# A transformer layer's first loads in another order: Q and K weights first on one queue, two x tiles on the scalar queue, no touching read

## The chip, the cores and the metric

The kernel runs on one core of one Trainium2 chip. A core has five engines that run side by side, each in the order of its own program: TensorE (PE, matmuls and transposes, its weight loads shown as PEld), VectorE (DVE), ScalarE (ACT), GpSimd (POOL) and SyncE (SP), which here only issues DMAs. ACT and POOL can issue DMAs too. Work is handed from engine to engine by semaphores. The metric is the device time of one execution in microseconds; the kernel before takes 264.89 us, the median of 3 runs from 264.78 to 264.89.

## The reference

With `x` of 2048 rows by 640 columns, the result is the sum of three terms: x itself, an attention over a few neighbours, and a gated feed-forward.

```python
x = A_x                                  # 1 x 2048 x 640, bf16
xn = (x - mean(x)) / sqrt(var(x) + 1e-5) # layer norm, no weights
q, k, v = split(xn @ wqkv)               # wqkv 640 x 1920, 32 heads of 20
# position s attends to s, s-2, ..., s-14; negative positions masked
logits = sum_d q[s] * k[s - 2w] * 20**-0.5      # w = 0..7
o = sum_w softmax_w(logits) * v[s - 2w]
A = o @ wo                               # 640 x 640
h = (xn @ w_gate) * (xn @ w_up)          # 640 x 1536 each
B = h @ w_down                           # 1536 x 640
return x + A + B
```

## The kernel before, in words

The 2048 rows are 16 tiles of 128 rows; the 640 columns are 5 chunks of 128 (`NCH`). For the attention and the feed-forward, four tiles make a block `j` of 512 rows.

**A planner writes the order.** The kernel doesn't state an order of instructions. Each piece of work is a Python generator (a thread) that yields `Task`s: an engine, a priority, what it reads and writes, and how many PSUM banks it needs. `Sched.run` (line 237) keeps a clock for each engine and an expected end for each instruction, takes at each step the task that can start first (among nearly equal ones that of the smallest priority), and appends its instructions. `Sched.op` (line 130) computes those expected ends from an `occ` written at each instruction; for a DMA an expected landing can be written by hand as `land=`. These figures only decide the order. Afterwards `emit` puts the instructions into the five programs and derives the semaphore waits from what each reads and writes. So another expected landing, or another cut of the work, can change the order of instructions far behind it.

**The front.** `x_load` (line 514) loads one tile of x, 160 KB. `wqkv_load(g, lo, hi)` (line 520) loads chunks lo to hi of the Q (g=0), K (1) or V (2) columns of `wqkv` as rows of 1280 bytes, 160 KB a chunk. The first loads are issued by hand at lines 1524 to 1532, all on SP but the touching read, a DMA on ACT's queue that reads 32 columns of every eighth row of Q's weights (5 KB) into a tile `TCH` that nothing uses. The order on SP is x tile 0, Q chunks 0 to 2, x tile 1, K chunks 0 to 2, Q chunks 3 and 4, x tile 2, K chunks 3 and 4; `loads` (line 524) goes on with x tiles 3 to 11, V's weights, and the rest.

`front(t)` (line 569) takes a tile through the layer norm and into its transposed form `XNT`: two half statistics and their aggregate on DVE (lines 577 and 580), the square root on ACT (587), the reciprocal on DVE (594), the normalisation on DVE (606 for tiles 0 and 1, in two parts, chunks 0 and 1 and chunks 2 to 4; 609 for the next; on ACT for later tiles). Tiles 0 to 3 are transposed on PE against an identity matrix (`trans`, line 640, instruction at 645) and copied from PSUM (656, 658 or 665); later tiles are transposed by DMA (678). For tiles 0 and 1 `trans` is one task with two banks: all five transposes stand together, and only the copies come in two parts. Three `warm` matmuls (line 683, on constants, their result unused) follow tile 0's transposes; ten longer ones stand at the very start.

`proj_group` (line 719) makes Q and K of a tile. For tiles 0 and 1 its inner function `spread` (line 722, matmuls at 733) works chunk by chunk, five matmuls of 128 rows for a chunk, and `STEPS` (line 506) says in which steps: chunks 0 and 1, chunk 2, chunks 3 and 4. Each step is a task of its own, so that a step can start when its weights and its chunk of `XNT` are there. Later tiles and V go through `mms` (line 693, matmuls at 701).

**Behind the front.** DVE multiplies Q with shifted K (884 and 933), POOL adds, PE sums over the heads' elements (1016), DVE and ACT make the softmax, DVE multiplies with shifted V (1195), POOL adds (1200), PE sums (1254, at the end of each block's additions), and meanwhile PE does the gate and up projections (1318) and at last the down projections with `wo` (1419 and 1470), which go out through DVE (1483) and DMA.

## Time and profile before

| what | value |
|---|---|
| median of 3 runs | 264.89 us (264.78 to 264.89) |
| the profiled execution's own time | 265.17 us |
| its span, first to last instruction | 263.4 us |
| PE busy | 259.6 us, 99% |
| DVE, POOL, ACT busy | 219.1, 160.5, 112.8 us |
| mean clock granted to PE | 1.000 |
| DMA, mean over the span | 151 GB/s |

The profiled execution is 0.28 us above the median; about 1.8 us of its time lie outside the span. A busy share is an average over the whole span, and a matmul's end is modelled, so 99% does not say that PE is at its peak; whether PE was held up is read from the chain of work and from the list of waits. In the views, "PE PS L733" is PE's work of line 733 that writes the tile PS, "x10" counts instructions, SPq and ACTq are the DMA issues of those engines, and what stands behind "<-" in brackets is what ended the idle time before. Intervals that share a row overlap: of pipelined matmuls the next one starts long before the last one's modelled end, so spacing is read from starts.

### The profile page before, as it was taken

What the parts mean: (1) busy time and instruction counts of PE and PEld (TensorE: products, weight loads), DVE (VectorE), ACT (ScalarE), POOL (GpSimd) and SP (SyncE); (2) the same over time, 40 slices, a digit from 0 to 9 for tenths busy, and PEclk for the clock granted to TensorE, in tenths of its full rate; (3) what the DMA queues carried; (4) which work ended last, traced back from release to release, by engine and by line L of the source; (5) the groups of instructions that cost most, each with busy time, mean ns of one, the idle gap of its engine ahead of it and who ended that gap; (6) DMA issues with size and microseconds to landing.
All of it is one profiled execution on the core that took longest, in us unless ns stands there. A gap on an engine that the chain in (4) does not pass through costs nothing.

```text
span 263.4 us, 4101 instructions
## 1 busy us (share of the span) xinstructions
PE 259.6 (99%) x1587; PEld 136.0 (52%) x1587; DVE 219.1 (83%) x259; ACT 112.8 (43%) x198; POOL 160.5 (61%) x97
## 2 busy tenths in 40 slices
PE   8999999999999999999999999999999999999996
PEld 3996964544444444444444444444444444445675
DVE  4798899999898798868779999999989989995041
ACT  3569987556622221224257665541324116211300
POOL 3000000000599999999983455899979999999300
PEclk9999999999999999999999999999999999999999
DMA  6985679933379996650249702566669865821621
GB/s 220 368 210 105 124 159 388 355 152 100 119 147 193 234 217 115 121 100 1 65 118 311 174 6 51 133 137 175 142 179 185 207 141 141 142 60 36 91 66 50
DMA packets 47843, 39.78 MB, mean 151 GB/s; under 512 B 23856, under 2 KB 45488, under 8 KB 47792
## 3 DMA queue, kind: packets, MB, share of 16 engines
q1 hardware_dynamic: 44848, 33.29, 48.4%
q0 software_dynamic: 2736, 6.16, 13.8%
q8 instruction: 12, 0.20, 0.3%
q10 hardware_dynamic: 240, 0.07, 0.1%
q14 instruction: 7, 0.06, 0.1%
HBM read 25.07 MB, written 7.23 MB: 123 GB/s over the span
## 4 chain that ended last, share of the span: by engine, by line
PE 96%; DMA 2%; SPq 0%; DVE 0%; issue 0%
PE PS L1318 39%; PE PS L701 23%; PE PS L1419 21%; PE PS L1470 7%; PE PS L1016 2%; DMA WQKV<-in_A_wqkv_dram 2%; PE PS L733 2%; PE PS L1254 2%; SPq L482 0%; PE PS L645 0%; DVE FB L1483 0%
## 5 line engine op out<-in xcount | busy, mean ns | idle before, releaser
L1200 POOL TENSOR_TENSOR SV<-PV 128x1024 bf16<-128x1024 f32 x40 | 94.1, 2524 | 17.8 <-DVE SM L1049 4.2
L1195 DVE TENSOR_TENSOR PV<-VX,PS 128x1024 f32<-128x1024 bf16 (+1 forms) x54 | 90.7, 1730 | 2.8 <-POOL SV L1200 2.8
L701 PE MATMUL PS<-XNT,WQKV 128*128 128x512 bf16 (+2 forms) x390 | 60.7, 316 | 0.0
L1318 PE MATMUL PS<-XNT,WG 128*128 128x512 bf16 x240 | 59.7, 379 | 0.0
L1318 PE MATMUL PS<-XNT,WU 128*128 128x512 bf16 x240 | 59.6, 379 | 0.0
L701 PEld LDWEIGHTS PS<-XNT,WQKV 128*128 128x128 bf16 x390 | 37.8, 112 | 21.9 <-ACT LOG L1027 0.8
L933 DVE TENSOR_TENSOR PRF<-PS,KT 128x1024 f32<-128x1024 f32 x32 | 38.0, 1218 | 0.3 <-PE PS L701 0.3
L1318 PEld LDWEIGHTS PS<-XNT,WG 128*128 128x128 bf16 x240 | 23.3, 98 | 28.7 <-issue 0.4
L1318 PEld LDWEIGHTS PS<-XNT,WU 128*128 128x128 bf16 x240 | 23.5, 98 | 28.3
L959 POOL TENSOR_TENSOR PRF<-PRF,PRF 128x1024 f32<-128x1024 f32 x8 | 21.0, 2634 | 21.6 <-DVE LOG L1076 21.6
L706 ACT ACTIVATE HT<-PS 128x512 bf16<-128x512 f32 x24 | 14.4, 598 | 35.4 <-PE PS L1318 35.4
L1419 PE MATMUL PS<-HT,WD 128*128 128x512 bf16 x120 | 27.5, 379 | 0.0
L884 DVE TENSOR_TENSOR PRD<-QT,KT 128x2048 bf16<-128x2048 bf16 x24 | 27.5, 1220 | 0.0
L706 ACT ACTIVATE UX<-PS 128x512 bf16<-128x512 f32 x15 | 9.0, 597 | 41.6 <-PE PS L1419 41.6
L1035 POOL MEMSET LOG<- 32x6 bf16 (+6 forms) x7 | 0.4, 95 | 42.8 <-ACT LOG L1027 42.8
L992 POOL TENSOR_TENSOR PRD<-PRF,PRF 128x1024 bf16<-128x1024 f32 x8 | 20.6, 2633 | 0.1
L970 POOL TENSOR_TENSOR PRF<-PRF,PRD 128x1024 f32<-128x1024 f32 x8 | 19.7, 2563 | 0.0
L1419 PEld LDWEIGHTS PS<-HT,WD 128*128 128x128 bf16 x120 | 11.7, 98 | 14.3 <-ACT OT L1263 0.4
L1419 PE MATMUL PS<-OT,WO 128*128 128x512 bf16 x75 | 18.6, 379 | 0.0
L1327 DVE TENSOR_TENSOR HT<-HT,PS 128x512 bf16<-128x512 bf16 x18 | 12.3, 686 | 7.2 <-PE PS L1318 7.1
L1483 DVE TENSOR_TENSOR FB<-PS,XR 128x320 bf16<-128x320 f32 (+2 forms) x9 | 4.1, 454 | 16.2 <-PE PS L1470 15.3
L577 DVE BATCH_NORM_STATS2 STATS<-XST 128x6 f32<-128x320 bf16 x32 | 14.2, 467 | 2.3 <-DMA XST<-in_A_x_dram 2.1
(76 smaller groups left out, 247.2 us busy)
## 6 DMA issues: line engine op xcount, KB each, us to landing
VX<-v_scratch SPq DMA_DIRECT2D x80, 130.0 KB, 3.0
PRF<-PRF POOLq DMA_DIRECT2D x8, 512.0 KB, 5.4
XST<-in_A_x_dram SPq DMA_DIRECT2D x16, 160.0 KB, 5.2
v_scratch<-VST SPq DMA_DIRECT2D x4, 640.0 KB, 6.4
WG<-in_B_w_gate_dram SPq DMA_DIRECT2D x1, 1920.0 KB, 8.8
WU<-in_B_w_up_dram SPq DMA_DIRECT2D x1, 1920.0 KB, 12.4
out_dram<-in_A_x_dram SPq DMA_DIRECT2D x1, 1920.0 KB, 18.1
WD<-in_B_w_down_dram SPq DMA_DIRECT2D x1, 1920.0 KB, 8.4
```

The costliest lines, as they stand in the source:

```text
L701: op("pe", (lambda o, l, x, c, first: lambda e: e.matmul(o, l, x, start=first, stop=(c == NCH - 1)))(o, l, x, c, first), r=[l, x], w=[o], ...
L706: X = op("act", (lambda o, i: lambda e: e.activation(o, i, ACT.Copy))(o, i), r=[i], w=[o], name=name, occ=0.12 + n * 0.9e-3)
L884: op("dve", lambda e: e.tensor_tensor(s[:], qb, kv, ALU.mult), r=[q, rk], w=[s[:]], name=f"prod{j}_{r}_{c}", occ=1.15, lock=True)
L933: X = op("dve", lambda e: e.tensor_tensor(o[:], qb, kv, ALU.mult), r=[q, rk, ("qev", j, c)], w=[o[:]], name=f"prow{j}_{r}_{c}_{q0}", occ=1.17)
L959: yield Task("pool", lambda: op("pool", lambda e: e.tensor_tensor(x, x, y, ALU.add), r=[x, y] + tokens(), w=[x], name=name, occ=2.36, lock ...
L970: yield Task("pool", lambda: op("pool", lambda e: e.tensor_tensor(x, x, z, ALU.add), r=[x, z] + tokens(), w=[x], name=name + "c", occ=2.36 ...
L992: yield Task("pool", lambda: op("pool", lambda e: e.tensor_tensor(o, a, y, ALU.add), r=[a, y] + tokens(), w=[o], name=f"qend{j}_{r}_{q0}", ...
L1195: last[0] = op("dve", lambda e: e.tensor_tensor(p, vw, a, ALU.mult), r=[vv] + rk, w=[p], name=f"pv{u}_{x}_{r0}", occ=0.09 + 1.1 * nr)
L1200: X = op("pool", lambda e: e.tensor_tensor(o, p[:, :, 0, :], p[:, :, 1, :], ALU.add), r=[p[:]] + tokens(), w=[o], name=f"pva{u}_{x}", occ= ...
L1318: op("pe", (lambda l, x, c: lambda e: e.matmul(PS[:, b, :], l, x, start=(c == 0), stop=(c == NCH - 1)))(l, x, c), r=[l, x], w=[PS[:, b, :] ...
L1419: op("pe", (lambda l, x, i: lambda e: e.matmul(PS[:, b, :], l, x, start=(i == 0), stop=(i == n - 1)))(l, x, i), r=[l, x], w=[PS[:, b, :]], ...
L1470: op("pe", (lambda l, x, i: lambda e: e.matmul(dst, l, x, start=(i == 0), stop=(i == n - 1)))(l, x, i), r=[l, x], w=[PS[:, b, :]], name=f" ...
```

## The change

Seven DMAs in place of eight at the start, in another order and on two queues; two structural cuts go with them.

- SP's first load is Q chunks 0 to 2, then K chunks 0 and 1, Q chunks 3 and 4, x tile 2, K chunks 2 to 4. K's first part is two chunks where it was three.
- x tiles 0 and 1 are issued by ACT, ahead of its table load. The touching read and its tile are gone.
- For tiles 0 and 1 each part's transposes are a task of their own with one bank, ready when that part is normalised. Tile 0's three warm matmuls follow the second part.
- For tile 0 the steps of the projections are chunks 0 and 1, chunk 2, chunk 3, chunk 4.
- The expected landings written at the loads, and ACT's starting time for the planner, are other numbers.

```diff
-    TCH = sb("TCH", [128, NCH, 32])
...
-    STEPS = (((0, 2), (2, 3), (3, NCH)), ((0, 2), (2, 3), (3, NCH)))
-
-    def part_of(t, c):
-        return next(k for k, (lo, hi) in enumerate(PARTS[t]) if lo <= c < hi)
+    STEPS = (((0, 2), (2, 3), (3, 4), (4, NCH)), ((0, 2), (2, 3), (3, NCH)))
...
-            def trans(*bs):
-                tpvs = [PS[:, b, :].bitcast(BF16)[:, 0:NCH * 128].rearrange("p (c f) -> p c f", c=NCH) for b in bs]
-                b, tpv = bs[0], tpvs[0]
-                for c in range(NCH):
-                    i, q = xs[:, c * 128:(c + 1) * 128], tpvs[part_of(t, c) if len(bs) > 1 else 0][:, c, :]
+            def trans(k, *bs):
+                hold.extend((b, PS[:, b, :].bitcast(BF16)[:, 0:NCH * 128].rearrange("p (c f) -> p c f", c=NCH)) for b in bs)
+                for c in range(*PARTS[t][k]) if t < N_SPLIT else range(NCH):
+                    i, q = xs[:, c * 128:(c + 1) * 128], hold[k][1][:, c, :]
                     op("pe", (lambda q, i: lambda e: e.transpose(q, i, IDENT[:]))(q, i), r=[i, IDENT[:]], w=[q],
                        name=f"tr{t}_{c}", occ=0.057, lat=0.2)
-                hold.extend(zip(bs, tpvs))
-                if t == 0:
-                    warm(3)
+                if t == 0 and k:
+                    warm(N_WARM)
...
-            yield Task("pe", trans, r=[xs], prio=p, banks=len(PARTS[t]) if t < N_SPLIT else 1)
             if t < N_SPLIT:
-                for k, e in enumerate(COPY[t]):
+                for k, ((lo, hi), e) in enumerate(zip(PARTS[t], COPY[t])):
+                    yield Task("pe", (lambda k: lambda *bs: trans(k, *bs))(k), r=[xs[:, lo * 128:hi * 128]], prio=p, banks=1)
                     yield Task(e, (lambda k, e: lambda: part(k, e))(k, e), r=[PS[:, hold[k][0], :]], prio=p - 1)
             else:
+                yield Task("pe", lambda b: trans(0, b), r=[xs], prio=p, banks=1)
...
+    N_WARM = 3
...
-    x_load(0, land=3.2)
-    tch = A_wqkv.rearrange("(c k p) n -> k c p n", k=16, c=NCH)[:, :, 0, 0:32]
-    stores.append(dma(TCH[0:16], tch, w=[TCH[0:16]], name="touch", eng="act"))
-    wqkv_load(0, 0, 3, land=5.1)
-    x_load(1, land=5.5)
-    wqkv_load(1, 0, 3, land=7.1)
-    wqkv_load(0, 3, NCH, land=8.0)
-    x_load(2, land=8.5)
-    wqkv_load(1, 3, NCH, land=9.6)
-    K.t["act"] = 2.1
+    wqkv_load(0, 0, 3, land=4.8)
+    x_load(0, eng="act", land=3.2)
+    x_load(1, eng="act", land=4.0)
+    wqkv_load(1, 0, 2, land=5.9)
+    wqkv_load(0, 3, NCH, land=6.8)
+    x_load(2, land=7.3)
+    wqkv_load(1, 2, NCH, land=8.6)
+    K.t["act"] = 2.95
     warm(10, JB)
```

## The prediction

> **What bounds the kernel now.** I read the page first, for the busy shares, then the chain that ended last, in order of time, then PE's waits, and last the timeline, the DMA issues and the stretches of the first 14 us, because everything that the change writes stands there.

> The page, engine line (share of the span, instructions):

> ```profile
> PE 259.6 (99%) x1587; PEld 136.0 (52%) x1587; DVE 219.1 (83%) x259; ACT 112.8 (43%) x198; POOL 160.5 (61%) x97
> ```

> The chain that ended last (start us, us, what):

> ```profile
> 2.26 5.14 DMA WQKV<-in_A_wqkv_dram
> ...
> 7.45 0.75 PE PS L733 x10
> 8.20 0.28 PE PS L645 x5
> 8.48 2.86 PE PS L733 x50
> ...
> 11.62 1.40 PE PS L733 x25
> ...
> 171.61 1.19 PE PS L1254 x20
> ```

> PE's waits (us in total, times, longest):

> ```profile
> PE PS L645 <- DVE XNS L606: 0.4, 1, 0.4
> PE PS L733 <- DMA WQKV<-in_A_wqkv_dram: 0.2, 1, 0.2
> ```

> The reader is to see that from 7.45 us on the chain is PE and nothing but PE until 261.16: no later wait of PE is listed at all. So the time is the moment at which PE's work starts to flow, plus a sum of matmuls that the change leaves as it is, plus what lies behind the last matmul. The change can win only in front of 11.2 us, and can lose there or by a wait that PE has nowhere now.

> The timeline of that stretch (start, us, engine, line, what; in brackets idle before):

> ```profile
> 0.82 0.40 SPq L482 DMA_DIRECT2D XST<-in_A_x_dram  x1
> 0.83 0.40 ACTq L482 DMA_DIRECT2D TCH<-in_A_wqkv_dram  x1
> ...
> 3.36 0.89 DVE L577 BATCH_NORM_STATS2 STATS<-XST 128x6 f32<-128x320 bf16 x2 [2.12 <-DMA XST<-in_A_x_dram]
> ...
> 6.26 1.00 PE L733 MATMUL PS<-XNT,WQKV 128*128 128x128 bf16 x15
> ...
> 7.45 0.75 PE L733 MATMUL PS<-XNT,WQKV 128*128 128x128 bf16 x10 [0.19 <-DMA WQKV<-in_A_wqkv_dram]
> 8.04 0.44 PE L645 MATMUL PS<-IDENT,XNS 128*128 128x128 bf16 x5
> 8.35 2.99 PE L733 MATMUL PS<-XNT,WQKV 128*128 128x128 bf16 x50
> ```

> Two chains meet. The first runs from the landing of x tile 0 through statistics, square root, normalisation, transposes and copy to the first projection at 6.26. The second is the K rows, issued fourth on SP at 2.26 and landed 5.14 later, at 7.40.

> DMA issues of two short windows there (KB, us from issue to landing), and the stretches (last column GB/s):

> ```profile
> XST<-in_A_x_dram SPq DMA_DIRECT2D x1, 160.0 KB, 2.5
> TCH<-in_A_wqkv_dram ACTq DMA_DIRECT2D x1, 5.0 KB, 2.3
> ```

> ```profile
> 2.50:3.00 0.50, 0.50 (x3) 0.20 (x2) 0.00 (x0) 0.04 (x1) 0.36 (x3) 1.00 1.15 217
> 3.00:3.50 0.50, 0.50 (x3) 0.22 (x2) 0.14 (x1) 0.00 (x0) 0.31 (x3) 1.00 0.63 197
> 3.50:4.00 0.50, 0.50 (x3) 0.16 (x2) 0.50 (x2) 0.00 (x0) 0.31 (x2) 1.00 1.07 397
> ```

> The DMA engines run at half their rate until about 3.25 us and at 315 to 397 GB/s from there on; the clock granted to PE is 1.00 throughout.

> **The change part by part.**

> *The loss that is there to be won.* From 6.26 to the transposes of tile 2 at 11.18 PE issues 75 projection matmuls and 5 transposes. At 1.40/25 = 0.056 us each (chain, 11.62) these are 80 x 0.056 = 4.48 us; the stretch is 4.92, so 0.44 is lost. Of it 0.35 is the K wait: 15 matmuls from 6.26 end at 7.10, the next starts at 7.45 (the 0.19 in the brackets counts from the modelled end of the last matmul).

> *K rows in two chunks, Q's second part ahead of them.* In the built program PE now does Q chunks 0 to 2 of tile 0 (15), Q chunks 3 and 4 (10), two transposes of tile 1, K chunks 0 and 1 (10), three transposes, then tile 1. K's first rows are thus wanted at about 7.8 instead of 7.10, and are 320 KB instead of 480, issued second on SP instead of fourth: that wait goes. Late next is Q's second part (320 KB, issued third on SP), wanted at 7.10, with everything on PE queued behind it.

> *Transposes in two parts.* PE reaches the first two at 6.26 + 25 x 0.056 = 7.66. In tile 0 the first transpose came 0.40 behind the start of the normalisation (5.05 to 5.45); in tile 1 that starts at 7.29, so 7.69: 0.03 lost. Then 0.11 of transposes, 0.56 of K and 0.17 of transposes end at 8.53. The copy of three chunks on ACT started 0.20 behind the last transpose (8.04 + 0.28 to 8.52) and took 0.49: 9.22, about 9.28 for PE. In between lie only the 10 matmuls that need the other copy: 8.53 + 0.56 = 9.09. So 0.19 are lost that before were covered. Bounds: 0 (ACT's copy starts at once) to 0.25. Together 0.22 lost against 0.44: a gain of 0.22, if the loads keep up.

> *x tiles 0 and 1 on the scalar queue.* ACT issues two DMAs of 0.40 to 0.49 (SP's rows) from 0.83, then the table load of 1.28 that stands at 1.26 now: it ends about 3.0, and the first square root is at 4.52. Cover 1.5 us, cost nothing. Tile 1's earlier landing buys nothing: DVE takes it at 5.60, behind tile 0's normalisation, and it had landed by 5.4. SP's later issues move up by two places, about 1 us; the engines, not the issues, set those landings.

> *Tile 0 beside Q's 480 KB.* Both are now issued at 0.82. Not shown before. Low end: 0.2 us earlier, since 5 KB need 2.3 where tile 0 needs 2.5. High end: all 480 KB go first, 480/380 = 1.26 us later. A fair share costs 160/380 = 0.42, and while tile 0 moved alone the engines ran at 203 to 217 of 397 GB/s, so about half of that was free: I take 0.18 late. The nearest row, the touching read beside tile 0 on the other queue, is at the low side: tile 0 took 2.5 all the same. [...]

> *Q's second part.* Now (before) 1440 KB behind tile 0 land between 3.25 and 8.34 (issued 2.74, 5.6 to landing): 3.5 ns per KB. The first weights are issued 0.45 earlier, so full rate starts at about 2.8, and ahead of this landing lie tile 1, Q, K and itself, 160 + 480 + 320 + 320 = 1280 KB, 4.5 us: 7.3. Bounds: 7.1 (no wait) if the whole half-rate stretch fills, to 7.86 if nothing moves up (landings of 7.40 at 1280 KB and 8.34 at 1600, interpolated at 1440). So 0.2 late, 0 to 0.76.

> *Half of tile 3's statistics ahead of tile 2's reciprocal* (the planner's new order on DVE). It needs tile 3, landed at 4.26 + 5.9 = 10.16 before, 9.71 if the stream is 0.45 earlier. From that half statistic to the transposes of tile 2 it takes 0.45 + 0.90 (10.28 to 11.18) = 1.35: 11.06. PE is there at 11.18 - 0.22 = 10.96. So 0.1 late, bounds 0 to 0.55.

> *No touching read.* What the first weight rows cost without it no row shows. Bounds: a gain of 0.1 (the 5 KB leave the engines to tile 0), to 0.5 us lost (the stretch 3.00 to 3.50, in which the first weights start and the engines move half of what they move next, once more). I take nothing, since tile 0, which nothing touches first, lands in 2.5, and the 5 KB in 2.3.

> *Further back.* The order differs: V's matmuls swap places, softmax of the second pair moves up on DVE, and the sums of block 0 (171.61, line 1254) stand three groups of five matmuls earlier, 15 x 0.216 = 3.24 us. POOL's tenth addition for them ended at 164.46 + 4.66 = 169.12; the sums would come at 168.4 less the gain. If DVE and POOL are not earlier, that is a wait of 0.75 to 1.0. They are: the softmax, which held DVE at 140.24 behind a product of 2.2, needs copies that ACT ended at 136.27. I take nothing.

> **Sum.** The late loads run side by side, so the largest counts, not their total: -0.22 + 0.2 (Q's second part; tile 0's 0.18 and tile 3's 0.1 lie inside) = -0.02. On the profiled execution, 265.17 (span 263.4 and 1.8 around it), 265.15; it lies 0.28 above the median of 264.89, so 264.87, which I round to 264.85.

> **Rivals.** 0.2% of 264.89, about what a measurement of this kernel can tell from no change, is 0.53.
> [...]
> 2. *The weights come late without the touch, or in the third place*: Q's second part past 7.85. At 8.1: 264.89 - 0.22 + 1.0 = 265.65. For it: the 0.5 us gap; against: they are issued 0.45 to 1 us earlier.
> 3. *A new order breaks behind*: sums of block 0 wait 0.75 to 1.0: 264.89 + 0.55 to 0.8, near 265.55. Against it: DVE's earlier softmax.
> 4. *All loads are early*: tile 0 by 0.2, no wait for Q's second part, no gap at the copy: -0.44 - 0.2 = -0.64, 264.25. For it: the idle engines until 3.25; against: it needs all three.
> 5. *It does nothing*: only the K wait moves to another load. That is my forecast.

> **Chances.** Forecast 0.55 (its own range 264.45 to 265.35), rival 1 0.13, 2 0.12, 3 0.05, 4 0.15. Faster by over 0.2% is rival 4, 0.15; slower are 1 to 3, 0.30; within, 0.55. Range 264.3 to 265.65: the bounds of the loads, up to the price of rivals 1 and 2, leaving out the outer part of each.

> **What would show it.** Right: no PE wait on K at 7.1; PE's first projection at 6.3 to 6.5; a short wait on WQKV between 15 and 10 matmuls, one on ACT's copy of 0.2; tile 2's transposes at 11.0 to 11.3; from there PE without a gap. Wrong: DVE's first statistics past 4.1, or a PE wait beyond 30 us.

## The result and the profile after

The kernel after takes 265.62 us (median of 9 executions, 265.31 to 267.33) against 264.91 (264.78 to 265.20) for the kernel before on the same chip: a ratio of 1.0045, 95% interval 1.0027 to 1.0063. It is slower, by 0.27% to 0.63%. The nine are not one cloud: five lie between 265.31 and 265.62, one at 266.28 and three between 267.26 and 267.33. The profiled one is of the upper group (267.28, span 265.5), and both groups need an explanation. Two executions of other series that were far slower than all the rest (343.21 and 707.79 us) are left out of the comparisons below.

The page of the kernel after, engine line (share of the span, instructions):

```profile
PE 261.2 (98%) x1587; PEld 137.2 (52%) x1587; DVE 218.7 (82%) x259; ACT 112.7 (42%) x198; POOL 160.6 (60%) x97
```

The same number of matmuls, but PE is busy 1.6 us longer than before, which no waiting explains. The chain that ended last, for the kernel after (start us, us, what):

```profile
0.83 3.52 DMA XST<-in_A_x_dram
...
4.38 0.90 DVE STATS L573 x2
...
6.47 0.79 PE PS L640 x5
7.26 0.64 PE PS L680 x3
7.90 2.25 PE PS L728 x25
10.15 0.11 PE PS L640 x2
10.26 0.56 PE PS L728 x10
...
13.44 0.28 PE PS L640 x5
...
171.55 1.19 PE PS L1249 x20
```

PE's waits of the kernel after (us in total, times, longest):

```profile
PE PS L640 <- DVE XNS L602: 1.2, 1, 1.2
```

Before, the chain ran through K's rows and through PE from 7.45 on. Now it starts with x tile 0, and the wait on K's rows is gone from the list. The only wait of PE in its list behind its launch is the one for tile 0's normalisation, 1.2 us where it was 0.4. The sums of block 0 start at 171.55 (171.61 before) without a wait.

The timeline of the kernel after (start, us, engine, line, what; in brackets the idle time before), and the issues of its first microsecond (KB, us from issue to landing):

```profile
0.82 1.51 SPq L481 DMA_DIRECT2D WQKV<-in_A_wqkv_dram  x3
0.83 0.95 ACTq L481 DMA_DIRECT2D XST<-in_A_x_dram  x2
...
4.38 0.89 DVE L573 BATCH_NORM_STATS2 STATS<-XST 128x6 f32<-128x320 bf16 x2 [3.14 <-DMA XST<-in_A_x_dram]
...
7.70 2.45 PE L728 MATMUL PS<-XNT,WQKV 128*128 128x128 bf16 x25
...
13.28 0.44 PE L640 MATMUL PS<-IDENT,XNS 128*128 128x128 bf16 x5
```

```profile
WQKV<-in_A_wqkv_dram SPq DMA_DIRECT2D x1, 480.0 KB, 4.5
XST<-in_A_x_dram ACTq DMA_DIRECT2D x1, 160.0 KB, 3.5
```

Two things went wrong, one on top of the other.

**x tile 0 is late.** It took 3.5 us instead of 2.5 from issue to landing, so DVE's first statistics start at 4.38 and not at 3.36: 1.02 us.

**PE runs at half rate.** The first 25 projections take 2.25 us, 90 ns each on average and 107 at their start, where 25 took 1.40 (56 ns each) before. Against the full rate, read from an execution that had it (the chain of the kernel with 13 warm matmuls, below: 0.63 for the five transposes, 0.33 for the three short warm matmuls, 1.40), this costs 0.16 + 0.31 + 0.85 = 1.32 us.

Less the 0.22 that the forecast gave to the cuts, 1.02 + 1.32 - 0.22 = 2.12. In the timeline tile 2's transposes stand at 13.28 against 11.18, 2.10 later; the span grew by 2.1; the profiled executions differ by 267.28 - 265.17 = 2.11.

The stretches in which x tile 0 is loaded (the last column is GB/s):

```profile
2.00:2.50 0.50, 0.50 (x2) 0.15 (x1) 0.00 (x0) 0.50 (x1) 0.24 (x2) 1.00 0.66 44
2.50:3.00 0.50, 0.50 (x3) 0.21 (x2) 0.00 (x0) 0.50 (x1) 0.36 (x3) 1.00 0.66 189
3.00:3.50 0.50, 0.50 (x3) 0.22 (x2) 0.00 (x0) 0.10 (x1) 0.32 (x3) 1.00 1.03 341
```

With two large transfers issued together the engines moved less at first, not more: 44 and 189 GB/s, where the kernel before moved 203 and 217. Only from 3.0 on they moved more (341 for 197).

### The profile page after: what moved, and what is told of

It is laid out like the page before. It is cut to its first block, busy times and chain, and to the rows that moved or that the text cites. A ratio compares the mean times of both kernels' runs of the same rounds, so it can differ in the third digit from the quotient of the medians.

```text
span 265.5 us, 4100 instructions
## 1 busy us (share of the span) xinstructions
PE 261.2 (98%) x1587; PEld 137.2 (52%) x1587; DVE 218.7 (82%) x259; ACT 112.7 (42%) x198; POOL 160.6 (60%) x97
## 4 chain that ended last, share of the span: by engine, by line
PE 97%; DMA 1%; DVE 1%; ACT 0%; issue 0%
PE PS L1313 39%; PE PS L696 23%; PE PS L1414 21%; PE PS L1465 7%; PE PS L728 2%; PE PS L1011 2%; PE PS L1249 2%; DMA XST<-in_A_x_dram 1%; PE PS L640 1%; DVE STATS L573 0%; PE PS L680 0%; DVE XNS L602 0%; ACT SD L583 0%; DVE FB L1478 0%; DVE MV L576 0%
## 5 line engine op out<-in xcount | busy, mean ns | idle before, releaser
L987 POOL TENSOR_TENSOR PRD<-PRF,PRF 128x1024 bf16<-128x1024 f32 x8 | 21.3, 2699 | 0.1
```

What stands on the lines that cost most here:

```text
L987: yield Task("pool", lambda: op("pool", lambda e: e.tensor_tensor(o, a, y, ALU.add), r=[a, y] + tokens(), w=[o], name=f"qend{j}_{r}_{q0}", ...
```

## The experiments

Every number of the kernel before is from the same chip and the same series as the kernel it is compared with. Landings of x tile 0 are issue plus duration in the one profiled execution of each kernel.

### Which part of the loading makes x tile 0 late

The first three runs ask whether it is the neighbour on the other queue, the missing touching read, or ACT's queue.

**x tile 0 on SP, ahead of Q's rows.**

```diff
+    x_load(0, land=3.2)
     wqkv_load(0, 0, 3, land=4.8)
-    x_load(0, eng="act", land=3.2)
     x_load(1, eng="act", land=4.0)
```

> x tile 0 goes first on SP, ahead of Q's rows; x tile 1 stays on ACT's queue; still no touching read; all else as in the kernel after. Theory sharing (x tile 0 is late because Q's 480 KB are issued at the same moment on the other queue): x tile 0 lands at 3.3 to 3.7 us, DVE's first statistics start there, total 264.6 to 265.0. Theory touch (it is late because nothing touched the rows first): it lands at 4.0 or later, total as after, 265.3 to 265.6. Theory ACT queue (a first load on ACT's queue is late by itself): 3.3, total as under sharing.

Measured: 266.06 us against 265.21, ratio 1.0043 (1.0026 to 1.0060), x tile 0 at 3.67. The landing is the one that sharing named, the time is not: another load had become the last one. Its chain:

```profile
2.27 5.89 DMA WQKV<-in_A_wqkv_dram
```

This is Q's second part, landed at 8.15. PE started its projections at 6.67, was through the first 15 at 6.67 + 15 x 0.056 = 7.51 and went on at 8.20. From 4 to 6 us the engines of this execution moved 298 to 300 GB/s, where the kernel before moved 367 to 376; why is not settled. x tile 1 still stood on ACT's queue at the same moment as x tile 0, and beside its 160 KB x tile 0 took 2.9 us, although it was on SP and issued 0.01 us ahead.

**The kernel before without the touching read.**

```diff
     x_load(0, land=3.2)
-    tch = A_wqkv.rearrange("(c k p) n -> k c p n", k=16, c=NCH)[:, :, 0, 0:32]
-    stores.append(dma(TCH[0:16], tch, w=[TCH[0:16]], name="touch", eng="act"))
     wqkv_load(0, 0, 3, land=5.1)
```

> The kernel before without the touching read, nothing else changed. Sharing and ACT queue: x tile 0 lands at 3.2 to 3.4 us as before, total within 0.2 us of before. Touch: x tile 0 or the first Q rows land 0.5 us or more later, total 265.4 or more.

Measured: 265.06 against 265.21, ratio 0.9999 (0.9990 to 1.0007). The issue of x tile 0 in this kernel:

```profile
XST<-in_A_x_dram SPq DMA_DIRECT2D x1, 160.0 KB, 2.3
```

Nothing is late without the touching read; x tile 0 landed at 3.08 in place of 3.33, and Q's first rows took 3.8 us (3.7 before). K's rows landed at 6.86 in place of 7.40 and PE didn't wait for them, yet the total is the same; what that says of the kernel before stands further down.

**The touching read put back.**

```diff
+    TCH = sb("TCH", [128, NCH, 32])
...
     wqkv_load(0, 0, 3, land=4.8)
+    tch = A_wqkv.rearrange("(c k p) n -> k c p n", k=16, c=NCH)[:, :, 0, 0:32]
+    stores.append(dma(TCH[0:16], tch, w=[TCH[0:16]], name="touch", eng="act"))
     x_load(0, eng="act", land=3.2)
```

> The kernel after with the 5 KB touching read put back as ACT's first DMA, ahead of x tile 0, which is thereby issued about 0.45 us later. Touch: x tile 0 lands at 3.8 or earlier although issued later, total below 265.2. Sharing and ACT queue: it lands no earlier than after's 4.35, total 265.3 to 266.0.

Measured: 268.96 against 265.21, ratio 1.0138 (1.0107 to 1.0169), far above every range. The chain of this kernel:

```profile
1.29 3.92 DMA XST<-in_A_x_dram
```

Issued 0.46 later, x tile 0 landed 0.85 later than in after, at 5.20. So the touching read is neither the cause nor a cure, and here the tile issued behind Q's rows took longer, 3.9 us from issue to landing, than the one issued beside them in after, 3.5.

**The two queues exchanged.**

```diff
-    wqkv_load(0, 0, 3, land=4.8)
-    x_load(0, eng="act", land=3.2)
-    x_load(1, eng="act", land=4.0)
+    wqkv_load(0, 0, 3, eng="act", land=4.8)
+    x_load(0, land=3.2)
+    x_load(1, land=4.0)
```

> The kernel after with the two queues exchanged at the start: x tiles 0 and 1 on SP, Q chunks 0 to 2 on ACT, all at the same moment as in after. Theory sharing (x tile 0 is late because another large transfer is issued at the same moment on the other queue): x tile 0 lands at 3.7 to 4.4 us as in after, total no better than 265.3. Theory ACT queue (a first load on ACT's queue is late by itself): x tile 0 lands at 3.1 to 3.4, as it did on SP in the kernel before, and Q's rows are the late ones; the total may still be late by Q's second part.

Measured: 265.56 (the median of six executions) against 265.00, ratio 1.0026 (1.0014 to 1.0038). In the profiled execution (265.25) x tile 0 landed at 3.28, although Q's 480 KB were issued beside it. Sharing as I had put it is refuted: the same two transfers at the same moment don't make x tile 0 late when it is the one on SP. That execution waited 0.25 for Q's second part, which landed at 7.33; what the slower ones waited for no profile shows.

### The cuts alone, and the four corners

**The change's cuts with the loads of the kernel before.**

```diff
+    TCH = sb("TCH", [128, NCH, 32])
...
-    wqkv_load(0, 0, 3, land=4.8)
-    x_load(0, eng="act", land=3.2)
-    x_load(1, eng="act", land=4.0)
-    wqkv_load(1, 0, 2, land=5.9)
-    wqkv_load(0, 3, NCH, land=6.8)
-    x_load(2, land=7.3)
-    wqkv_load(1, 2, NCH, land=8.6)
-    K.t["act"] = 2.95
+    x_load(0, land=3.2)
+    tch = A_wqkv.rearrange("(c k p) n -> k c p n", k=16, c=NCH)[:, :, 0, 0:32]
+    stores.append(dma(TCH[0:16], tch, w=[TCH[0:16]], name="touch", eng="act"))
+    wqkv_load(0, 0, 3, land=5.1)
+    x_load(1, land=5.5)
+    wqkv_load(1, 0, 2, land=6.7)
+    wqkv_load(0, 3, NCH, land=7.7)
+    x_load(2, land=8.2)
+    wqkv_load(1, 2, NCH, land=9.6)
+    K.t["act"] = 2.1
```

> The kernel after's cuts (transposes in two parts, K's first rows in two chunks, Q's second part third of the weights) with the loads as in the kernel before: x tile 0 first on SP, the touching read on ACT, then Q chunks 0 to 2, x tile 1, K chunks 0 and 1, Q chunks 3 and 4. If only the two queues were wrong (x tile 0 beside Q's rows): first projection at 6.26, Q's second part wanted at 7.1 and landed near 7.4, total 0.1 above to 0.2 below before's. If Q's second part behind K's first rows is a fault of its own: it lands at 7.9 or later, PE waits 0.8 us or more, total 0.5 us or more above before's.

Measured: 264.89 against 265.00, ratio 0.9995 (0.9987 to 1.0004). The timeline of this kernel:

```profile
3.33 0.89 DVE L574 BATCH_NORM_STATS2 STATS<-XST 128x6 f32<-128x320 bf16 x2 [2.09 <-DMA XST<-in_A_x_dram]
...
6.22 1.56 PE L729 MATMUL PS<-XNT,WQKV 128*128 128x128 bf16 x25
...
8.27 2.40 PE L729 MATMUL PS<-XNT,WQKV 128*128 128x128 bf16 x40
...
10.51 0.44 PE L641 MATMUL PS<-IDENT,XNS 128*128 128x128 bf16 x5
```

PE runs from 6.22 on without a wait for weights. In this order 70 projections stand ahead of tile 2's transposes, not 75, so 10.51 answers to 10.51 + 5 x 0.056 = 10.79 with 75, where the kernel before has 11.18. DVE started 0.03 earlier, so against that one execution of the kernel before the cuts win 0.36: the whole wait for K, since in this planner's order the gap at the copy doesn't open. In the total (0.11, interval from 0.34 faster to 0.11 slower) that is at the edge of what 11 executions tell.

On this kernel, in which nothing else is late, the two suspected conditions were set apart: which queue x tile 0 is on, and whether Q's 480 KB are issued at the same moment on the other one. PE's order of work is the same in all four.

x tile 0 on ACT, Q's rows 0.45 us later on SP, behind the 5 KB read:

```diff
-    x_load(0, land=3.2)
+    x_load(0, eng="act", land=3.2)
...
-    stores.append(dma(TCH[0:16], tch, w=[TCH[0:16]], name="touch", eng="act"))
+    stores.append(dma(TCH[0:16], tch, w=[TCH[0:16]], name="touch", eng="sp"))
```

> The kernel with the cuts only, with x tile 0 and the touching read exchanged between the queues: x tile 0 first on ACT, the 5 KB read first on SP, Q's rows second on SP, about 0.45 us after x tile 0. PE's order is unchanged. Theory simultaneous (x tile 0 is late when Q's 480 KB are issued at the same moment on the other queue, whichever queue it is on): x tile 0 lands at 3.1 to 3.4 us, total as with the cuts only, 264.7 to 265.1. Theory ACT queue (x tile 0 is late on ACT's queue by itself): 3.7 to 4.4, total 265.2 to 265.9, above 266.5 where the clock comes late. Theory both needed: as simultaneous.

x tile 0 on SP, Q's rows at the same moment on ACT:

```diff
     x_load(0, land=3.2)
-    tch = A_wqkv.rearrange("(c k p) n -> k c p n", k=16, c=NCH)[:, :, 0, 0:32]
-    stores.append(dma(TCH[0:16], tch, w=[TCH[0:16]], name="touch", eng="act"))
-    wqkv_load(0, 0, 3, land=5.1)
+    wqkv_load(0, 0, 3, eng="act", land=5.1)
```

> The kernel with the cuts only, x tile 0 first on SP as there, Q chunks 0 to 2 first on ACT at the same moment, no touching read. Theory simultaneous: x tile 0 at 3.7 to 4.4 us, total 265.2 to 265.9. Theory ACT queue, and theory both needed: x tile 0 at 3.1 to 3.4, total 264.7 to 265.1.

x tile 0 on ACT, Q's rows at the same moment on SP, as in after:

```diff
-    x_load(0, land=3.2)
-    tch = A_wqkv.rearrange("(c k p) n -> k c p n", k=16, c=NCH)[:, :, 0, 0:32]
-    stores.append(dma(TCH[0:16], tch, w=[TCH[0:16]], name="touch", eng="act"))
+    x_load(0, eng="act", land=3.2)
     wqkv_load(0, 0, 3, land=5.1)
```

> The kernel with the cuts only, x tile 0 first on ACT, Q chunks 0 to 2 first on SP at the same moment, as in after, no touching read. All three theories: x tile 0 at 3.7 to 4.4 us, total 265.2 to 265.9 and in some executions above 266.5. If it lands before 3.5, x tile 1 on ACT behind x tile 0, which this kernel has not, is part of the cause.

The issues of the first microsecond, of the kernel with x tile 0 on ACT and Q later, of the one with x tile 0 on SP and Q beside it on ACT, and of the one with x tile 0 on ACT and Q beside it on SP:

```profile
XST<-in_A_x_dram ACTq DMA_DIRECT2D x1, 160.0 KB, 2.3
TCH<-in_A_wqkv_dram SPq DMA_DIRECT2D x1, 5.0 KB, 2.0
```

```profile
WQKV<-in_A_wqkv_dram ACTq DMA_DIRECT2D x1, 480.0 KB, 4.1
XST<-in_A_x_dram SPq DMA_DIRECT2D x1, 160.0 KB, 2.5
```

```profile
WQKV<-in_A_wqkv_dram SPq DMA_DIRECT2D x1, 480.0 KB, 4.3
XST<-in_A_x_dram ACTq DMA_DIRECT2D x1, 160.0 KB, 3.0
```

| x tile 0 on | Q's rows | x tile 0 landed, us | total, us | ratio to before |
|---|---|---|---|---|
| SP | later | 3.30 | 264.89 (264.71 to 265.21) | 0.9995 (0.9987 to 1.0004) |
| ACT | later | 3.17 | 264.87 (264.69 to 265.20) | 0.9992 (0.9983 to 1.0000) |
| SP | same moment, on ACT | 3.28 | 265.01 (264.69 to 265.12) | 0.9994 (0.9986 to 1.0003) |
| ACT | same moment, on SP | 3.80 | 267.12 (265.21 to 267.82) | 1.0066 (1.0042 to 1.0090) |

The first row is of another series (the kernel before: 265.00) than the other three (265.09). Neither condition alone costs anything; with both, five of six executions stand at 266.87 to 267.82. The landing of 3.80 belongs to the sixth, the fastest (265.21); the five have no profile. The other profiles with both conditions (after, and after with 16 and with 13 warm matmuls, below) show 4.35, 3.71 and 3.90. So the first two lines of the new order are enough for the whole of the loss, and the cuts are harmless. That the rest of the new order of loads is harmless isn't shown: the first two kernels that took x tile 0 to SP, with the later loads in after's order, were slower than the one before as well (266.06 and 265.56), and in both profiles PE waited for Q's second part.

### Is it the queue or the order of issue?

With both conditions, Q's issue on SP stands at 0.82 and x tile 0's on ACT at 0.83. Either ACT's transfer gives way to SP's, or the later one gives way to the earlier. The next kernel, again the cuts only with other first loads, issues x tile 0 on SP behind Q's rows on ACT:

```diff
-    x_load(0, land=3.2)
     tch = A_wqkv.rearrange("(c k p) n -> k c p n", k=16, c=NCH)[:, :, 0, 0:32]
-    stores.append(dma(TCH[0:16], tch, w=[TCH[0:16]], name="touch", eng="act"))
-    wqkv_load(0, 0, 3, land=5.1)
+    stores.append(dma(TCH[0:16], tch, w=[TCH[0:16]], name="touch", eng="sp"))
+    x_load(0, land=3.2)
+    wqkv_load(0, 0, 3, eng="act", land=5.1)
```

> The kernel with the cuts only, with Q chunks 0 to 2 first on ACT, and on SP the 5 KB read first and x tile 0 second, so that x tile 0 is issued on SP about 0.45 us behind Q's rows. Theory order (whichever transfer is issued first is served first, and in after Q's rows were issued a hundredth of a microsecond ahead): x tile 0 lands at 4.8 to 5.3 us, total 266.0 or more. Theory queue (ACT's transfer gives way to SP's, however they were issued): x tile 0 lands 2.3 to 2.6 behind its issue, at 3.6 to 3.9, total 265.0 to 265.4.

Measured: 267.97 against 264.99, ratio 1.0111 (1.0098 to 1.0124). Q's rows on ACT (issued at 0.83) and x tile 0 on SP (issued at 1.28):

```profile
WQKV<-in_A_wqkv_dram ACTq DMA_DIRECT2D x1, 480.0 KB, 3.8
XST<-in_A_x_dram SPq DMA_DIRECT2D x1, 160.0 KB, 3.8
```

x tile 0 landed at 5.04, as the theory of order said and the theory of queues excluded. Until 3.1 us SP's queue moved 96 packets, all under 512 B, as many as the 5 KB read has in the kernel before, and none of x tile 0, while Q's move from 1.97 on: with 0.45 us between the issues the transfer on SP did not go first here, the earlier one did.

For the 0.01 us of after this settles nothing, and the packets there fit neither theory. The profile counts them by queue (q1 is SP's, q10 ACT's; packets, MB, share of the 16 engines); a tile of x is 128 of them. From 1.5 to 2.5 us, the kernel before, in which ACT's packets are those of the 5 KB, and after:

```profile
q1 hardware_dynamic: 89, 0.11, 42.1%
q10 hardware_dynamic: 43, 0.00, 2.9%
```

```profile
q10 hardware_dynamic: 25, 0.03, 49.6%
```

From 2.2 to 2.6 us, the kernel with x tile 0 on SP and Q beside it on ACT, and the one with x tile 0 on ACT and Q beside it on SP:

```profile
q1 hardware_dynamic: 86, 0.10, 83.6%
q10 hardware_dynamic: 6, 0.01, 22.0%
```

```profile
q10 hardware_dynamic: 22, 0.03, 54.8%
```

After from 2.6 to 3.1 us:

```profile
q1 hardware_dynamic: 50, 0.06, 44.9%
q10 hardware_dynamic: 50, 0.06, 35.3%
```

In after all 25 packets until 2.5 us are x tile 0's; Q's first one starts at 2.53. So x tile 0 goes first there too, but slowly: over this 1 us the 16 engines spent 0.496 x 16 / 25 = 0.32 us on a packet, where the kernel before needed 0.421 x 16 / 89 = 0.08. From 2.6 to 3.1 both queues start equally many. Its loss is slow first packets and then a shared stretch, not a place behind Q's rows. Why the first packets are slow with x tile 0 on ACT and Q's 480 KB on SP, and not with the queues exchanged, the runs don't show. In all these kernels the transfer on SP is also the one issued 0.01 us ahead, so at this distance a part of the queue can't be told from a part of the order.

**A third of the amount beside it**, against the kernel with x tile 0 on ACT and Q beside it on SP.

```diff
     x_load(0, eng="act", land=3.2)
-    wqkv_load(0, 0, 3, land=5.1)
+    wqkv_load(0, 0, 1, land=4.2)
+    wqkv_load(0, 1, 3, land=5.1)
```

> The kernel with x tile 0 first on ACT and Q first on SP at the same moment, but Q's first load is one chunk of 160 KB, and its chunks 1 and 2 follow as a second load 0.4 us later. If x tile 0's lateness grows with the rows that the other queue has at that moment: it lands at 3.2 to 3.5 us, total 264.8 to 265.2. If any large transfer at the same moment does it, or what counts is all that SP issues in the first microsecond: 3.7 to 4.4, total 265.2 and up, with executions near 267.

Measured: 265.38 against 264.99, ratio 1.0020 (1.0009 to 1.0032), one of 12 executions at 267.11. The two transfers of equal size:

```profile
WQKV<-in_A_wqkv_dram SPq DMA_DIRECT2D x1, 160.0 KB, 3.0
XST<-in_A_x_dram ACTq DMA_DIRECT2D x1, 160.0 KB, 3.1
```

They landed within 0.14 of each other, at 3.82 and 3.96: they shared. Here Q's packets were ahead, 66 to 28 until 2.6 us. x tile 0 is no earlier than beside 480 KB (3.71 to 4.35), so in these profiles its lateness does not follow the size of the other load; what it follows within that range stays open.

### The upper group: PE's clock

**Sixteen warm matmuls for ten.**

```diff
-    warm(10, JB)
+    warm(16, JB)
```

> The kernel after with 16 long warm matmuls at the start in place of 10, so that PE's idle time before the first transposes shrinks from 1.2 us to almost nothing. Theory clock (the executions near 267.3 us come from PE running at half rate until about 9.6 us, because of that idle time): all executions at 265.3 to 265.7, projections 56 ns apart in every profile. If the idle time has nothing to do with it: again two groups, 265.4 and 267.3. x tile 0 lands at 4.35 in either case.

Measured: 267.27 (267.02 to 267.98) against 265.21. This was no test of the clock: the planner counts the warm matmuls too, and it put tile 0's last three transposes behind tile 1's chain, so PE stood idle until 8.06. It showed one thing by the way: PE had reached the full rate before, and after an idle time of 1.95 us the projections still ran at it, 56 ns each.

**Thirteen, with the planner's clock set back,** to see whether the group near 267.3 stays when PE's idle time ahead of the first transposes, 1.2 us in after, is shorter.

```diff
     warm(10, JB)
+    t_pe = K.t["pe"]
+    warm(3, JB)
+    K.t["pe"] = t_pe
```

> The kernel after with 13 long warm matmuls at the start in place of 10, and the planner's clock for PE set back, so that all that follows keeps after's order on every engine. At half rate 13 take 5.5 us and end by 6.4, about where the first transposes stand, so PE has no idle time of a microsecond. [...]

Measured: 265.48, 11 executions between 265.26 and 265.72, against 265.00; ratio 1.0017 (1.0009 to 1.0026). The group near 267.3 is gone (none of 11, where after had 3 of 9). The chain of this kernel:

```profile
0.83 3.06 DMA XST<-in_A_x_dram
...
6.01 0.29 PE PS L640 x2
6.30 0.34 PE PS L640 x3
6.64 0.33 PE PS L680 x3
6.97 1.40 PE PS L728 x25
```

x tile 0 is late as in after: DVE starts at 3.92, 0.56 behind the kernel before. But PE runs at full rate. In the timeline tile 2's transposes start at 11.55, 0.37 behind, so the cuts gave 0.19 back; the total is 0.48 above.

The kernel with x tile 0 second on SP shows the clock itself, in its stretches (the third number from the right is the clock granted to PE):

```profile
6.00:7.00 1.00, 0.00 (x0) 0.00 (x0) 0.60 (x3) 0.29 (x1) 0.00 (x0) 1.00 1.02 369
7.00:8.00 1.00, 0.84 (x7) 0.62 (x8) 1.00 (x4) 0.39 (x2) 0.00 (x0) 0.51 1.05 373
...
9.00:10.00 1.00, 1.00 (x13) 1.00 (x11) 0.63 (x2) 0.00 (x0) 0.00 (x0) 0.50 1.07 374
10.00:11.00 1.00, 1.00 (x17) 1.00 (x16) 0.00 (x0) 0.00 (x0) 0.00 (x0) 0.79 1.07 365
```

There the trace's records of the clock stand at 3.60 (full), 7.01 (half) and 10.43 (full), 3.41 us apart; PE was idle from 4.52 to 7.16, and the clock fell. In after the first record of the full clock is at 9.56, in the kernel before at 4.60, in the one with x tile 0 on SP at 6.28. What the clock follows no view shows. What stands here is an estimate, from these records and from PE's work in the timelines, in steps of 3.41 us counted back from the first record. In after the step from 2.73 to 6.15 held PE's work only until 5.28, 75%, and the clock was at half behind it; the one from 6.15 to 9.56 held 90%, and it was full behind it. With x tile 0 on SP 2.87 to 6.28 held 85%, with x tile 0 second 0.19 to 3.60 held 80%, with the cuts only 0.15 to 3.56 held 79%, and it was full behind each; with the touching read put back 6.50 to 9.92 held 76%, and it was at half (first record at 13.33). The kernel before has 0.45 us of idle time in that place, 13% of a step, and none of its 30 executions beside the kernel with 13 was above 265.21.

The mean granted clock of the single executions fits this. A clock that rises and falls back for one step of 3.41 us, as in the profiled execution with x tile 0 second, gives 1 - 0.5 x 3.41/265.5 = 0.994, and so it reads in two of the five slow executions of the kernel with x tile 0 on ACT and Q beside it on SP (267.82 and 267.23), in two of six with the touching read put back and in three of four with x tile 0 second on SP; no execution below 267 reads so. A clock that is late with its first rise left no such sign: after reads 1.000 in its upper group too, with the first record at 9.56 in its profiled execution.

### Two tries at a better kernel

**Q's second part ahead of K's first.** All loads on SP, no touching read, in the order x tile 0, Q chunks 0 to 2, x tile 1, Q 3 and 4, K 0 and 1, x tile 2, K 2 to 4.

```diff
-    wqkv_load(0, 0, 3, land=4.8)
-    x_load(0, eng="act", land=3.2)
-    x_load(1, eng="act", land=4.0)
-    wqkv_load(1, 0, 2, land=5.9)
-    wqkv_load(0, 3, NCH, land=6.8)
-    x_load(2, land=7.3)
-    wqkv_load(1, 2, NCH, land=8.6)
-    K.t["act"] = 2.95
+    x_load(0, land=3.1)
+    wqkv_load(0, 0, 3, land=5.0)
+    x_load(1, land=5.4)
+    wqkv_load(0, 3, NCH, land=6.6)
+    wqkv_load(1, 0, 2, land=7.4)
+    x_load(2, land=7.9)
+    wqkv_load(1, 2, NCH, land=9.4)
+    K.t["act"] = 2.1
```

> All loads on SP, no touching read, after's cuts, and the order in which the cuts want the rows: x tile 0, Q chunks 0 to 2, x tile 1, Q chunks 3 and 4, K chunks 0 and 1, x tile 2, K chunks 2 to 4. If both faults named (two queues at once, Q's second part behind K's first) are the causes: x tile 0 lands at 3.1 to 3.3, Q's second part by 7.0, K's by 7.8, no wait of PE on weights, total 0.1 to 0.4 us below before's. If the cuts themselves cost (the new order of the work behind, or the gaps at tile 1's transposes): total at or above before's although no load is late.

Measured: 265.06 against 265.00, ratio 1.0002 (0.9993 to 1.0010). x tile 0 landed at 3.12 and PE waits for no load. But PE is in its warm matmuls until 5.28, so the first projection moves only from 6.26 to 6.06; tile 2's transposes start at 10.91, 0.27 earlier than in the profile of the kernel before, and the total doesn't show it. That total was to mean that the cuts cost by themselves, but the profile shows no such cost: its execution took 264.90, 0.27 less than the profiled one of the kernel before (265.17), which stood 0.26 above the median of its own series (264.91).

**Nine warm matmuls**, with the cuts only and no touching read, against the kernel with the cuts only.

```diff
-    tch = A_wqkv.rearrange("(c k p) n -> k c p n", k=16, c=NCH)[:, :, 0, 0:32]
-    stores.append(dma(TCH[0:16], tch, w=[TCH[0:16]], name="touch", eng="act"))
...
-    warm(10, JB)
+    warm(9, JB)
+    K.t["pe"] += 0.427
```

> The kernel with the cuts only, without the touching read, and with 9 long warm matmuls in place of 10. x tile 0 lands at 3.1 and PE is free at 4.86, so the first projection starts at 6.1 in place of 6.38: total 264.4 to 264.8. If the clock needs the tenth matmul, some executions are 0.5 us or more above.

Measured: 264.90 against 265.09, ratio 0.9993 (0.9985 to 1.0002), so no better than the cuts alone. PE started its transposes at 5.25, but at half rate (0.64 us in the chain for the three short warm matmuls, 0.33 with 13), and the first projection stood at 6.47, where it was at 6.22 with the cuts only. No kernel of the study beats the one before by more than its measurement can tell.

## Why the prediction was wrong

I forecast no change, 264.85 within 264.45 to 265.35, or 264.3 to 265.65 with part of the rivals. The time is 265.62, slower by 0.27% to 0.63%: outside the first range and only just inside the second. The loss is at tile 0's loading, the place of rival 1 (chance 0.13), with PE's clock beside it, which I hadn't seen.

- **The step that failed is "Tile 0 beside Q's 480 KB", taken as 0.18 late.** It was 1.02 late in the profiled execution and 0.38 to 0.57 in the three other profiles with the tile on ACT and the 480 KB beside it on SP (3.71, 3.80 and 3.90 against 3.33), inside the bounds of -0.2 to 1.26. I leaned on the touching read as the nearest row, which left tile 0 at 2.5. But it was 5 KB, and its row could not price 480. I also read the half-rate stretch until 3.25 as free capacity; with two transfers it became slower still (44 GB/s for 203), though until 2.5 us only the tile's own packets moved. The fair share, 160/380 = 0.42, was the better figure: 264.89 - 0.22 + 0.42 = 265.1. It is an estimate from the kernel before alone, and what the runs show of sharing is mixed: from 2.6 to 3.1 us after's two queues started 50 packets each, and where Q was issued 0.45 us ahead on ACT, none of the tile's 128 started before 3.1.
- **Rival 1, a late x tile 0, came true in its place; that all of Q's rows go first, my high end of 1.26 us, did not.** Tile 0 was late and all hung on it, but its packets were the first. One us late gives 264.89 - 0.22 + 1.0 = 265.7, and that this is near the median of 265.62 is luck: the one execution known to be one us late took 267.28, with the clock's part. The equal issue times (0.82 and 0.83) were half of the condition: the same two transfers cost nothing with x tile 0 on SP and Q on ACT (ratio 0.9994), or with Q 0.45 us later (0.9992).
- **What no step held: PE's clock.** I wrote that the granted clock "is 1.00 throughout". That column says 1.00 in after too, from 7 to 9.5 us, while projections start 107 ns apart: it is filled with 1.00 up to the first record. The ten warm matmuls of the kernel before, 4.15 us for ten of 512 columns against 0.216 for one later on, already said that PE starts at half rate. Idle time of PE there has a second price, 1.32 us in the profiled execution and, by their times, in two more of the nine.
- **The loss to be won was right for the profiled execution, and not for the median**: 0.22 worked out, 0.19 with 13 warm matmuls, 0.36 in the order of the kernel with the cuts only, where the gap at the copy is missing. K's wait is in no list of the kernels with the cuts; the gap at the three-chunk copy, worked out as 0.19, is 0.17 of idle weight loads in after. But I took this off the median, and the profiled execution of the kernel before, 265.17, is not a median one. In the seven profiles with 75 projections ahead of tile 2's transposes (both kernels and five of the experiments) the time less the start of these transposes is 253.96 to 254.00. By that, an estimate, they start near 264.91 - 253.98 = 10.93 in a median execution and not at 11.18, and 0.25 of the 0.44 was not there to be won. The kernel before without the touching read agrees: no wait for K, and the same total.
- **Q's second part, 7.3 (7.1 to 7.86), was right**: 7.58 in after, 7.34 with 13 warm matmuls, 7.37 with the cuts only. PE did not wait for it in after, because tile 0 was later still.
- **No touching read, taken as nothing, was right** (ratio 0.9999), and so rival 2 fell. One landing past my bound, 8.15, was seen with x tiles 0 and 1 issued together.
- **The order further back, taken as nothing, was right**: no wait of PE for another engine or a load behind 13.3 us, in any list. The sums of block 0 stand ten matmuls earlier, though, 2.16 us, and not the 15 and 3.24 that I counted: 420 gate and up matmuls are ahead of them in after's chain, 430 before.
- **The signs named were the right ones**: DVE's first statistics past 4.1 was to show the forecast wrong, and they stood at 4.38.

## What to carry to other kernels

Where a chain of small dependent steps hangs on one load, issue that load alone or clearly first: moving the two x tiles to ACT's queue saved their issues on SP (0.40 and 0.49 us), and a load of 480 KB issued 0.01 us ahead on SP cost the first of them 0.4 to 1.0 us; one issued 0.45 us ahead cost it 1.3 and 1.4 (3.8 and 3.9 us for 2.5). A row of a small transfer doesn't price a large one; between far bounds, take the fair share unless a row with two large transfers says otherwise. Where warm matmuls are there to raise PE's clock, count the idle time behind them as a loss of clock as well as of time (here 1.32 us beside the 1.02 of the late tile), and read the clock from the distance of matmuls, not from its column ahead of the first record. Where a gain of some tenths is read from one profiled execution, first see how far that execution lies from the median.
